# Low parts of the feed-forward activations on VectorE instead of GpSimd, and a lighter last group of block 1

## The chip, the cores and the metric

The kernel runs on one core of one Trainium2 chip. The metric is the device time of one execution in microseconds (us); a change is judged by the medians of runs before and after. The engines are named as in the profile: PE is TensorE (PEld its weight loads), DVE is VectorE, ACT is ScalarE, POOL is GpSimd, SP issues the DMAs. Each engine takes its own instructions strictly in the order in which they were written; engines wait for one another through semaphores.

## What is computed

Clustered attention (2 batches, 8 heads, 768 tokens, head size 64) gives x of 1536 tokens by 512. Two feed-forward blocks follow, and only these are touched:

```python
    x = np.ascontiguousarray(attn_out.transpose(0, 2, 1, 3)).reshape(B * S, H * D)
    x = _moe_ref(x=x, **moe_kwargs)          # block 1
    return _moe2_ref(x=x, **moe2_kwargs)     # block 2
...
    h = x @ w_in                                         # 512 -> 2048
    g = np.maximum(h, 0.0) + np.log1p(np.exp(-np.abs(h)))
    return (g @ w_out).astype(np.float32)                # 2048 -> 512
...
    g = x @ w_gate                                       # 512 -> 1536
    silu = g * (1.0 / (1.0 + np.exp(-g)))
    val = x @ w_val
    return (silu * val @ w_out).astype(np.float32)       # 1536 -> 512
```

## The kernel before

**Products in three passes.** A matrix product is made from operands split in a rounded high part and a low part (value minus high part): high by high, high by low, low by high, all added up in one PSUM bank. So each activation tile has a pair, gh and gl (block 1's g), YH and YL (block 1's output, which is block 2's input), ah and al (block 2's silu times val). The high part is a copy by ACT; the low part is a subtraction that must wait for that copy. Before the change gl and al (each 128x1536) are subtracted by POOL.

**Weights** come by DMA as 64-bit floats, in tiles of 128x512, and are narrowed to 32 bits and split: one ACT instruction (`m`, L123), then on DVE L125 and L128 (`m`), L132 and L135 (`m`), L148 (`whi`) and L149 (`wlo`). These steps lie as tasks in a list, `todo`; `pump()` emits one, two or three of them, by how many are left. There are two `m` buffers, so the ACT step of one weight waits for the `wlo` of the weight before the last. `need(...)` emits tasks until the named weight or activation is there.

**Block 1** has 16 units (`h_unit(f)`): 36 matmuls of 128x512 into three banks (L756), which ACT and DVE empty into `e` and `r` (L815, L819; L817 by DVE in units 0 to 2); then ACT's Exp and Ln (L822, L823), the sum `e` (DVE, L826), and the split into gh (ACT, L796) and gl (L797), these three as tasks in `todo`. After two units `y_group(g)` multiplies both by w_out (L845): four times (`d` from 0 to 3) 18 matmuls into three banks, which DVE adds to `acc` (L859; in the first group ACT copies them, L857), and a `pump()` after each `d`. In the last group each bank's result is also copied to YH (ACT, L861) and subtracted to YL (L863, by DVE or POOL).

**Block 2** has 12 units (`a_unit(f)`), with gate and val products (L756), and six `o_group`s (L944), emptied by DVE (L954, L956).

**Banks.** There are eight PSUM banks, used in turn, three for a unit or a `d`. So the third bank of a set is the one that was first in the set two sets before, and a set's third matmul waits until ACT or DVE has emptied that one (its first two banks were second and third in the set three sets before). The order of the code is the order on each engine.

Of the kernel before, what the change touches and what calls it, by code (L numbers as in the profile page):

```python
# [16 lines left out]
ALU = mybir.AluOpType  # L17
# [12 lines left out]
def _r(t):  # L30

    return t.bitcast(F32)
# [8 lines left out]
def kernel(  # L41
# [18 lines left out]
    nc = tc.nc  # L60
# [8 lines left out]
    KD = DM // 128  # L69
# [128 lines left out]
    def split_tasks(batch):  # L198

        steps = {}  # L200

        def first(key):
            while key not in loaded_t:
                load_ahead(len(loaded_t) + 1)
            steps[key] = w_narrow(loaded_t.pop(key))
            next(steps[key])

        def second(key):
            next(steps[key])

        def third(key, tag):
            x = next(steps[key])
            load_ahead(3)
            pool, bufs = pool_of[tag]
            W[key] = w_split(x, pool, tag, bufs)

        tasks = []
        for key, _, tag in batch:
            tasks.append(functools.partial(first, key))
            firsts.add(tasks[-1])  # L220
            tasks.append(functools.partial(second, key))
            begun.add(tasks[-1])
            tasks.append(functools.partial(third, key, tag))
            begun.add(tasks[-1])
        return tasks
# [11 lines left out]
    def pump(n=None):  # L237
        for _ in range(n or (3 if len(todo) > 12 else 2 if len(todo) > 4 else 1)):
            if todo and todo[0] in firsts:
                todo.popleft()()  # L240
            if todo:
                todo.popleft()()
            if todo and todo[0] in firsts and n is None:
                todo.popleft()()

    def need(table, key):
        while key not in table:
            todo.popleft()()
        return table[key]
# [393 lines left out]
    for half in range(2):  # L643
# [5 lines left out]
        for hh in range(2):  # L649
            g = 2 * C * hh  # L650
            if half == 0:
                nc.vector.tensor_scalar(
                    out=QT[hh][64:64 + C, 0, cols], in0=_r(ps)[g:g + C, 0:384], scalar1=FAR, scalar2=-FAR,
# [3 lines left out]
            else:  # L657
                nc.scalar.copy(KT[hh][64:64 + C, 0, cols], _r(ps)[64 + g:64 + g + C, 0:384])
                nc.scalar.activation(
                    out=QT[hh][64:64 + C, 0, cols], in_=_r(ps)[g:g + C, 0:384], func=AF.Identity,  # L660
# [84 lines left out]
    def bank():  # L745
        pool = bank_pools[bank_n[0] // 4 % len(bank_pools)]
        bank_n[0] += 1
        return pool.tile([128, 512], F32, tag="b", name="bank")

    def proj(xh, xl, w, banks, kks):  # L750

        hi, lo = w
        for kk in kks:
            for wt, xt, last in ((hi, xh, 0), (hi, xl, 0), (lo, xh, 1)):
                for c in range(NCH):
                    nc.tensor.matmul(  # L756
                        banks[c],
                        lhsT=wt[:, kk, :],
                        rhs=xt[:, kk, 512 * c:512 * c + 512],
                        start=(kk == 0 and wt is hi and xt is xh),  # L760
                        stop=(kk == KD - 1 and last == 1),
                    )
# [30 lines left out]
    def split_g(g, tag):  # L793
        gh = gp.tile([128, NTOK], F32R, tag="gh", name=tag + "h")
        gl = gp.tile([128, NTOK], F32R, tag="gl", name=tag + "l")
        nc.scalar.copy(gh, g)  # L796
        nc.gpsimd.tensor_tensor(out=gl, in0=g, in1=_r(gh), op=ALU.subtract)  # L797
        return gh, gl


# [32 lines left out]
    def y_group(g):  # L833
        last = g == NF1 // 2 - 1
        nd = 1
        for d0 in range(0, KD, nd):
            banks = [bank() for _ in range(nd * NCH)]
            for ff in range(2):
                hi, lo = need(W, ("out", 2 * g + ff))
                gh, gl = need(g_t, 2 * g + ff)  # L840
                for d in range(nd):
                    ds_ = slice(128 * (d0 + d), 128 * (d0 + d) + 128)
                    for n, (wt, gt) in enumerate(((hi, gh), (hi, gl), (lo, gh))):
                        for c in range(NCH):
                            nc.tensor.matmul(  # L845
                                banks[NCH * d + c],
                                lhsT=wt[:, 0, ds_],
                                rhs=gt[:, 512 * c:512 * c + 512],
                                start=(ff == 0 and n == 0),
                                stop=(ff == 1 and n == 2),  # L850
                            )
            for n, bk in enumerate(banks):
                d, c = d0 + n // NCH, n % NCH
                cs = slice(512 * c, 512 * c + 512)
                a = acc[:, d, cs]
                if g == 0:
                    nc.scalar.copy(a, bk)  # L857
                else:
                    nc.vector.tensor_tensor(out=a, in0=bk, in1=a, op=ALU.add)  # L859
                if last:  # L860
                    nc.scalar.copy(YH[:, d, cs], a)  # L861
                    eng = nc.gpsimd if c == 1 or c == 2 and d < KD - 1 else nc.vector
                    eng.tensor_tensor(out=YL[:, d, cs], in0=a, in1=_r(YH)[:, d, cs], op=ALU.subtract)  # L863
            pump()

    soft0, split0 = h_unit(0, h0)
    soft1, split1 = h_unit(1, h1)
# [2 lines left out]
    for g in range(NF1 // 2):  # L870
        if 2 * g + 2 < NF1:
            for f in (2 * g + 2, 2 * g + 3):
                soft, split = h_unit(f)
                if f < NF1 - 2:
                    todo.extend([soft[0]] + split[:3] + [soft[1]] + split[3:6] + [soft[2]] + split[6:])
                else:
                    first_do(soft + split[:3])
                    todo.extend(split[3:])
        else:
            YH = keep.tile([128, KD, NTOK], F32R, tag="xh", name="YH")  # L880
            YL = keep.tile([128, KD, NTOK], F32R, tag="xl", name="YL")
        y_group(g)
# [6 lines left out]
    def a_unit(f):  # L889
        gb = [bank() for _ in range(NCH)]  # L890
        wg = need(W, ("gate", f))
        vb = None
        if f == 0:
            vb = [bank() for _ in range(NCH)]
            wv = need(W, ("val", f))
            proj(YH, YL, wg, gb, range(KD - 1))
            proj(YH, YL, wv, vb, range(KD - 1))
            proj(YH, YL, wg, gb, range(KD - 1, KD))
            proj(YH, YL, wv, vb, range(KD - 1, KD))
        else:  # L900
            for half in range(2):
                proj(YH, YL, wg, gb, range(2 * half, 2 * half + 2))
                pump()
        sg = tp.tile([128, NTOK], F32, tag="e", name="sg")
        for c in range(NCH):
            cs = slice(512 * c, 512 * c + 512)
            nc.scalar.activation(out=sg[:, cs], in_=gb[c], func=AF.Silu)
        if vb is None:
            vb = [bank() for _ in range(NCH)]
            wv = need(W, ("val", f))  # L910
            for half in range(2):
                proj(YH, YL, wv, vb, range(2 * half, 2 * half + 2))
                pump()
        ah = gp.tile([128, NTOK], F32R, tag="gh", name="ah")
        al = gp.tile([128, NTOK], F32R, tag="gl", name="al")
        for c in range(NCH):
            cs = slice(512 * c, 512 * c + 512)
            nc.vector.tensor_tensor(out=sg[:, cs], in0=vb[c], in1=sg[:, cs], op=ALU.mult)  # L918
            if f == NF2 - 1:
                nc.scalar.copy(ah[:, cs], sg[:, cs])  # L920
                nc.vector.tensor_tensor(out=al[:, cs], in0=sg[:, cs], in1=_r(ah)[:, cs], op=ALU.subtract)

        def split_part():
            nc.scalar.copy(ah, sg)  # L924
            nc.gpsimd.tensor_tensor(out=al, in0=sg, in1=_r(ah), op=ALU.subtract)  # L925
            a_t[f] = (ah, al)

        if f < NF2 - 1:
            todo.append(split_part)
        else:  # L930
            a_t[f] = (ah, al)
        if batches:
            todo.extend(split_tasks(batches.pop(0)))

    def o_group(g):
        for t0 in range(0, NTOK // 128, 4):
# [22 lines left out]
            pump()  # L959

    a_unit(0)
    a_unit(1)
    for g in range(NF2 // 2):
        if 2 * g + 2 < NF2:
            a_unit(2 * g + 2)
            a_unit(2 * g + 3)
        o_group(g)
# [33 lines left out]
```

## Time and profile before

| what | us |
|---|---|
| median of 3 runs (lowest to highest) | 841.67 (839.91 to 848.4) |
| the profiled execution | 847.81 |
| its span, first to last instruction | 846.0 |

The profile is of one execution. Times in its rows count from the start of its span; block 1 lies from about 259 to 547 us and block 2 behind it. A row of an engine's time line gives the start, the duration, engine, line, operation, output and inputs, the count, and in brackets how long the engine had been idle before and who released it.

### The profile page before, as it was taken

The page shows a single profiled execution, that of the slowest core. Times are in us where ns is not written, and L with a number is a line of the kernel's source. Part 1 is how long each engine was busy: PE and PEld are TensorE (multiplying, and loading weights), DVE is VectorE, ACT ScalarE, POOL GpSimd, SP SyncE. Part 2 cuts the span into 40 slices and gives each one's busy share as a digit, 9 for nine tenths or more (in the row PEclk, how much of TensorE's full clock was granted, in tenths as well). Part 3 has the DMA queues.
Part 4 walks back from the last instruction along what each step waited for, and adds up shares of the span by engine and source line. Part 5 has one row for each costly group of instructions (what it writes and reads, how often), then busy time and mean ns, then how long its engine had stood idle before and what let it go on. Part 6 is the DMA issues. An engine that isn't in the chain of part 4 may idle for free.

```text
span 846.0 us, 11685 instructions
## 1 busy us (share of the span) xinstructions
PE 817.6 (97%) x4366; PEld 704.3 (83%) x4366; DVE 663.1 (78%) x1007; ACT 417.7 (49%) x774; POOL 240.7 (28%) x163
## 2 busy tenths in 40 slices
PE   7999999999999999999999999899999999999998
PEld 6999999999897778787787887688888888888886
DVE  6889988887895896989979789838885857766364
ACT  4589889888893776364553744233212112120210
POOL 4636455565421221212112313231111103011100
PEclk9699999999999989999999999999999999999999
DMA  8956765674411223122121120202311221310003
GB/s 213 262 134 143 197 148 147 147 170 113 103 31 54 75 75 100 50 77 74 60 90 51 50 76 26 74 1 78 121 52 49 76 74 50 100 51 25 1 1 149
DMA packets 65336, 75.42 MB, mean 89 GB/s; under 512 B 28960, under 2 KB 51584, under 8 KB 65280
## 3 DMA queue, kind: packets, MB, share of 16 engines
q1 hardware_dynamic: 65280, 74.68, 31.8%
q8 instruction: 34, 0.56, 0.3%
q14 instruction: 22, 0.18, 0.1%
HBM read 48.27 MB, written 3.19 MB: 61 GB/s over the span
## 4 chain that ended last, share of the span: by engine, by line
PE 75%; DVE 16%; DMA 4%; ACT 2%; issue 2%; POOL 1%; SPq 0%; POOLq 0%; DVEq 0%; ACTq 0%
PE bank L756 34%; PE bank L944 12%; PE bank L845 8%; PE ops L540 6%; PE sps L491 6%; PE tps L523 6%; DVE acc L859 3%; DVE whi L148 2%; DVE m L125 2%; PE sims L402 2%; DMA rd<-R 2%; DVE m L135 1%; DMA R<-rd 1%; DVE e L826 1%; DVE m L132 1%
## 5 line engine op out<-in xcount | busy, mean ns | idle before, releaser
L797 POOL TENSOR_TENSOR gl<-e,gh 128x1536 fp32r<-128x1536 f32 x16 | 59.9, 3746 | 204.7 <-ACT gh L796 191.6
L530 DVE TENSOR_TENSOR tl<-tps,th 128x384 fp32r<-128x384 f32 x192 | 98.8, 550 | 17.2 <-ACT th L529 16.8
L499 DVE TENSOR_REDUCE nm<-sps 128x1 f32<-128x768 f32 x96 | 91.4, 953 | 16.1 <-PE sps L491 13.3
L925 POOL TENSOR_TENSOR al<-sg,ah 128x1536 fp32r<-128x1536 f32 x11 | 38.6, 3507 | 207.0 <-ACT ah L924 207.0
L523 PE MATMUL tps<-id,p 128*128 128x128 f32 x576 | 95.4, 283 | 1.0 <-DVE tl L530 1.0
L529 ACT CAST th<-tps 128x384 fp32r<-128x384 f32 x192 | 84.7, 491 | 20.6 <-PE tps L523 18.0
L507 ACT ACTIVATE p<-sps,nm 128x768 f32<-128x768 f32 x96 | 88.3, 920 | 6.6 <-DVE nm L499 6.5
L491 PE MATMUL sps<-KT,QT 128*128 128x384 f32 x384 | 86.6, 348 | 4.1 <-ACT p L507 2.3
L756 PE MATMUL bank<-YH,whi 128*128 128x512 f32 x288 | 81.4, 390 | 3.3 <-DVE acc L859 3.3
L125 DVE TENSOR_SCALAR m<-m 128x512 f32<-128x512 f32 x68 | 58.9, 866 | 31.4 <-ACT m L123 31.3
L523 PEld LDWEIGHTS tps<-id,p 128*128 128x128 f32 x576 | 77.4, 154 | 7.2 <-DVE tl L530 3.4
L756 PE MATMUL bank<-YL,whi 128*128 128x512 f32 x288 | 81.5, 392 | 0.0
L756 PE MATMUL bank<-YH,wlo 128*128 128x512 f32 x288 | 81.4, 391 | 0.0
L540 PE MATMUL ops<-th,VV 128*128 128x256 f32 x288 | 80.6, 309 | 0.0
L123 ACT ACTIVATE m<-raw 128x512 f32<-128x512 f32 x68 | 44.5, 667 | 72.7 <-DVE wlo L149 72.7
L540 PE MATMUL ops<-tl,VV 128*128 128x256 f32 x288 | 73.1, 283 | 0.0
L918 DVE TENSOR_TENSOR sg<-bank,sg 128x512 f32<-128x512 f32 x36 | 22.8, 684 | 60.8 <-PE bank L756 60.8
L491 PEld LDWEIGHTS sps<-KT,QT 128*128 128x128 f32 x384 | 65.5, 196 | 5.4 <-ACT p L507 3.2
L845 PE MATMUL bank<-gh,whi 128*128 128x512 f32 x192 | 58.0, 407 | 11.0 <-DVE acc L859 6.6
L756 PEld LDWEIGHTS bank<-YH,whi 128*128 128x128 f32 x288 | 54.2, 188 | 15.0 <-issue 3.7
L756 PEld LDWEIGHTS bank<-YH,wlo 128*128 128x128 f32 x288 | 54.5, 189 | 11.4
L756 PEld LDWEIGHTS bank<-YL,whi 128*128 128x128 f32 x288 | 54.5, 189 | 11.3
(125 smaller groups left out, 1775.2 us busy)
## 6 DMA issues: line engine op xcount, KB each, us to landing
raw<-in_moe_w_out_dram SPq DMA_DIRECT2D x28, 512.0 KB, 3.4
raw<-in_moe_w_in_dram SPq DMA_DIRECT2D x16, 512.0 KB, 3.9
QT<-hi SPq DMA_DIRECT2D x32, 192.0 KB, 3.0
raw<-in_moe_w_val_dram SPq DMA_DIRECT2D x12, 512.0 KB, 3.9
raw<-in_moe_w_gate_dram SPq DMA_DIRECT2D x12, 512.0 KB, 3.4
KT<-hi SPq DMA_DIRECT2D x14, 384.0 KB, 4.9
qn<-in_q_dram SPq DMA_DIRECT2D x16, 192.0 KB, 4.4
kn<-in_k_dram SPq DMA_DIRECT2D x16, 192.0 KB, 4.0
```

The source lines that it names most:

```text
L125: nc.vector.tensor_scalar(out=m.bitcast(F32), in0=m.bitcast(F32), scalar1=F64_LEAST, scalar2=F64_MOST, op0=ALU.max, op1=ALU.min)
L491: nc.tensor.matmul(ps[:, c, 0:384], lhsT=Q[:, a, 128 * j:128 * j + 128], rhs=K[:, a, 384 * c:384 * c + 384], start=(a == 0), stop=(a == 1),)
L499: nc.vector.tensor_reduce(out=nm, in_=ps[:, :, 0:384], axis=AX.XY, op=ALU.max, negate=True)
L507: nc.scalar.activation(out=_h(p), in_=s_t.pop(i)[:, :, 0:384], func=AF.Exp, bias=nm_t.pop(i), accum_out=sm_t[pr][:, j:j + 1],)
L523: nc.tensor.transpose(ps[:, 128 * j:128 * j + 128], p[:, 128 * kb:128 * kb + 128], id32)
L529: nc.scalar.copy(th, pv)
L530: nc.vector.tensor_tensor(out=tl, in0=pv, in1=_r(th), op=ALU.subtract)
L540: nc.tensor.matmul(o[:, 0:CW], lhsT=VV_t[pr][:, hh, kb].rearrange("p a d -> p (a d)"), rhs=t[:, kb, :], start=(kb == 0 and lohi == 0), sto ...
L756: nc.tensor.matmul(banks[c], lhsT=wt[:, kk, :], rhs=xt[:, kk, 512 * c:512 * c + 512], start=(kk == 0 and wt is hi and xt is xh), stop=(kk ...
L797: nc.gpsimd.tensor_tensor(out=gl, in0=g, in1=_r(gh), op=ALU.subtract)
L845: nc.tensor.matmul(banks[NCH * d + c], lhsT=wt[:, 0, ds_], rhs=gt[:, 512 * c:512 * c + 512], start=(ff == 0 and n == 0), stop=(ff == 1 and ...
L944: nc.tensor.matmul(bk, lhsT=lhs[:, ts_], rhs=rhs[:, 0, :], start=(ff == 0 and n == 0), stop=(ff == 1 and n == 2),)
```

## The change

The two subtractions of gl and al go from POOL to DVE, at the same place in the code. In the last `y_group` no `pump()` is called, so nothing is narrowed there; `a_unit(0)` gets three `pump()`s between its products instead. And the subtraction that makes YL for one bank is emitted after the next bank has been added to `acc` and copied to YH, not right after its own.

```diff
         nc.scalar.copy(gh, g)
-        nc.gpsimd.tensor_tensor(out=gl, in0=g, in1=_r(gh), op=ALU.subtract)
+        nc.vector.tensor_tensor(out=gl, in0=g, in1=_r(gh), op=ALU.subtract)
...
         nd = 1
+        low = collections.deque()
...
                 if last:
                     nc.scalar.copy(YH[:, d, cs], a)
                     eng = nc.gpsimd if c == 1 or c == 2 and d < KD - 1 else nc.vector
-                    eng.tensor_tensor(out=YL[:, d, cs], in0=a, in1=_r(YH)[:, d, cs], op=ALU.subtract)
-            pump()
+                    low.append(functools.partial(
+                        eng.tensor_tensor, out=YL[:, d, cs], in0=a, in1=_r(YH)[:, d, cs], op=ALU.subtract
+                    ))
+                while len(low) > 1 or low and n == len(banks) - 1 and d0 == KD - nd:
+                    low.popleft()()
+            if not last:
+                pump()
...
             proj(YH, YL, wg, gb, range(KD - 1))
+            pump()
             proj(YH, YL, wv, vb, range(KD - 1))
+            pump()
             proj(YH, YL, wg, gb, range(KD - 1, KD))
             proj(YH, YL, wv, vb, range(KD - 1, KD))
+            pump()
...
             nc.scalar.copy(ah, sg)
-            nc.gpsimd.tensor_tensor(out=al, in0=sg, in1=_r(ah), op=ALU.subtract)
+            nc.vector.tensor_tensor(out=al, in0=sg, in1=_r(ah), op=ALU.subtract)
```

On DVE, in `y_group(1)` (banks of `d` 0, then of `d` 1 and 2), there stood before:

```order
L859 TENSOR_TENSOR acc<-bank,acc 128x512 x3
L826 TENSOR_TENSOR e<-r,e 128x1536
L125 TENSOR_SCALAR m<-m 128x512
L128 TENSOR_SCALAR m<-m 128x512
L132 SCALAR_TENSOR_TENSOR m<-raw,m 128x512
L135 SCALAR_TENSOR_TENSOR m<-raw,m 128x512
L148 CAST whi<-m 128x512
L149 TENSOR_TENSOR wlo<-m,whi 128x512
L859 TENSOR_TENSOR acc<-bank,acc 128x512 x3
L125 TENSOR_SCALAR m<-m 128x512
L128 TENSOR_SCALAR m<-m 128x512
L859 TENSOR_TENSOR acc<-bank,acc 128x512 x3
```

and after the change the stretch from the weight's last steps to the banks of `d` 2 reads:

```order
L148 CAST whi<-m 128x512
L149 TENSOR_TENSOR wlo<-m,whi 128x512
L860 TENSOR_TENSOR acc<-bank,acc 128x512 x3
L797 TENSOR_TENSOR gl<-e,gh 128x1536
L125 TENSOR_SCALAR m<-m 128x512
L128 TENSOR_SCALAR m<-m 128x512
L860 TENSOR_TENSOR acc<-bank,acc 128x512 x3
```

The gl of that unit now stands between the banks of `d` 1 and those of `d` 2; L859 has become L860.

On DVE in the last group, `y_group(7)`, there stood before, from the first bank of `d` 0 to the last YL:

```order
L859 TENSOR_TENSOR acc<-bank,acc 128x512 x2
L125 TENSOR_SCALAR m<-m 128x512
L128 TENSOR_SCALAR m<-m 128x512
L859 TENSOR_TENSOR acc<-bank,acc 128x512
L863 TENSOR_TENSOR YL<-acc,YH 128x512
L859 TENSOR_TENSOR acc<-bank,acc 128x512 x2
L132 SCALAR_TENSOR_TENSOR m<-raw,m 128x512
L135 SCALAR_TENSOR_TENSOR m<-raw,m 128x512
L148 CAST whi<-m 128x512
L149 TENSOR_TENSOR wlo<-m,whi 128x512
L859 TENSOR_TENSOR acc<-bank,acc 128x512
L863 TENSOR_TENSOR YL<-acc,YH 128x512
```

and now:

```order
L860 TENSOR_TENSOR acc<-bank,acc 128x512 x2
L868 TENSOR_TENSOR YL<-acc,YH 128x512
L860 TENSOR_TENSOR acc<-bank,acc 128x512 x3
L868 TENSOR_TENSOR YL<-acc,YH 128x512
L860 TENSOR_TENSOR acc<-bank,acc 128x512 x3
L868 TENSOR_TENSOR YL<-acc,YH 128x512
L860 TENSOR_TENSOR acc<-bank,acc 128x512 x3
L868 TENSOR_TENSOR YL<-acc,YH 128x512
L860 TENSOR_TENSOR acc<-bank,acc 128x512
L868 TENSOR_TENSOR YL<-acc,YH 128x512
L125 TENSOR_SCALAR m<-m 128x512
```

The six steps of one weight (the second gate tile, which `a_unit(1)` needs) have moved behind the whole group, and each YL stands one bank later. One weight load moves with them on SP's queue: `load_ahead` is called when a weight has been split. The order on PE and ACT is the same before and after.

## Rows read from the trace of the kernel before

**Rows 1.** The page: the chain that ended last, by engine

```profile
PE 75%; DVE 16%; DMA 4%; ACT 2%; issue 2%; POOL 1%; SPq 0%; POOLq 0%; DVEq 0%; ACTq 0%
```

**Rows 2.** Who PE waited for, 286 to 552: us in total, times, longest

```profile
PE bank L845 <- DVE acc L859: 6.6, 5, 1.8
PE bank L756 <- DVE acc L859: 4.2, 2, 3.3
PE bank L845 <- DVE r L817: 3.2, 1, 3.2
PE bank L845 <- DVE whi L148: 1.2, 1, 1.2
```

**Rows 3.** The chain in order of time, 286 to 552: start, us, what

```profile
298.14 19.07 PE bank L845 x70
317.21 16.32 PE bank L756 x72
...
348.04 5.53 PE bank L845 x16
...
384.43 3.92 PE bank L845 x16
...
422.39 16.16 PE bank L756 x70
...
453.05 5.52 PE bank L845 x16
...
547.27 4.76 PE bank L756 x14
```

**Rows 4.** The time line of PE, one of the waits

```profile
348.04 0.50 PE L845 MATMUL bank<-gh,whi 128*128 128x512 f32 x1 [1.82 <-DVE acc L859]
```

**Rows 5.** The time line of DVE, four places

```profile
297.41 1.87 DVE L817 TENSOR_SCALAR r<-bank 128x512 f32<-128x512 f32 x3
...
343.03 3.63 DVE L148 CAST whi<-m 128x512 fp32r<-128x512 f32 x1
...
347.31 1.88 DVE L859 TENSOR_TENSOR acc<-bank,acc 128x512 f32<-128x512 f32 x3
...
553.57 1.29 DVE L863 TENSOR_TENSOR YL<-acc,YH 128x512 fp32r<-128x512 f32 x1 [0.69 <-ACT YH L861]
```

**Rows 6.** The time line of POOL, three places

```profile
290.08 7.12 POOL L797 TENSOR_TENSOR gl<-e,gh 128x1536 fp32r<-128x1536 f32 x2 [30.82 <-ACT gh L796]
...
342.34 4.03 POOL L797 TENSOR_TENSOR gl<-e,gh 128x1536 fp32r<-128x1536 f32 x1 [9.31 <-ACT gh L796]
...
553.02 1.29 POOL L863 TENSOR_TENSOR YL<-acc,YH 128x512 fp32r<-128x512 f32 x1 [0.18 <-ACT YH L861]
```

**Rows 7.** Groups by line, 259 to 548 (last: 548 to 846): busy us, mean ns

```profile
L797 POOL TENSOR_TENSOR gl<-e,gh 128x1536 fp32r<-128x1536 f32 x16 | 59.9, 3746 | 204.7 <-ACT gh L796 191.6 <-PE bank L756 13.1
...
L826 DVE TENSOR_TENSOR e<-r,e 128x1536 f32<-128x1536 f32 x16 | 27.9, 1751 | 1.3 <-ACT e L823 1.3
...
L796 ACT CAST gh<-e 128x1536 fp32r<-128x1536 f32 x16 | 23.8, 1489 | 60.2 <-DVE e L826 60.2
...
L863 DVE TENSOR_TENSOR YL<-acc,YH 128x512 fp32r<-128x512 f32 x3 | 2.1, 692 | 2.1 <-ACT YH L861 2.1
...
L148 DVE CAST whi<-m 128x512 fp32r<-128x512 f32 x30 | 12.8, 427 | 1.0
```

**Rows 8.** The time line of ACT in `y_group(0)`

```profile
301.96 0.71 ACT L123 ACTIVATE m<-raw 128x512 f32<-128x512 f32 x1 [3.16 <-DVE wlo L149]
302.54 0.62 ACT L815 ACTIVATE e<-bank 128x512 f32<-128x512 f32 x1
```

**Rows 9.** Stretches: length, then busy of PE, PEld, DVE, ACT, POOL; clock, DMA

```profile
299.00:305.00 6.00, 6.00 (x16) 4.62 (x16) 5.45 (x11) 3.04 (x7) 0.00 (x0) 0.56 0.28 87
376.00:412.00 36.00, 34.18 (x152) 27.96 (x151) 33.07 (x40) 21.07 (x26) 10.46 (x3) 1.00 0.19 59
720.00:770.00 50.00, 50.00 (x222) 41.38 (x222) 35.32 (x57) 9.82 (x14) 7.03 (x2) 1.00 0.20 66
```

## The prediction, on record before the result

> **What bounds the kernel now.** I read first the chain that ended last [rows 1]: three quarters of it are PE and 16% are DVE, so PE is the bound and DVE delays it in places. The question is where, and whether the change touches those places. In block 2 the stretches show PE busy all the time, 50.00 of 50.00 us, with DVE at 35.32 [rows 9]: whatever al costs or saves there moves nothing as long as DVE keeps that slack. In block 1 PE does wait. The view of waits [rows 2] gives, from 286 to 552: 6.6 and 4.2 us for `acc` (a bank not yet emptied), 3.2 for `r`, 1.2 for `whi`: 15.2 us, all on DVE.
>
> Each wait costs more than its own length, which the chain shows [rows 3]. 72 matmuls of this shape take 16.32 us without a wait, 0.2267 each. The 16 that follow the wait at 348.04 [rows 4] take 5.53 instead of 3.63, so 1.90 are lost behind a wait of 1.82. In the same way 298.14 loses 19.07 - 70 x 0.2267 = 3.20, 384.43 loses 0.29, 422.39 0.29, 453.05 1.89, and 547.27 4.76 - 14 x 0.2267 = 1.59. The cause of the larger ones is the granted clock: 0.56 from 299 to 305, against 1.00 in the stretches around [rows 9], so PE stood at the lower of its two levels (1.2 instead of 2.4 GHz) for most of those 6 us, after 3.2 us of idling. Three shorter waits (525 to 540) I put at 0.3 each, by the rows that lose 0.29. Restarts cost 9.2 + 0.9 = 10.1 us. **So 25.3 us of block 1 are waits on DVE and their after-effects, and no more than about this can be won.**
>
> **Why DVE is late.** The mean of `whi` in block 2 is 427 ns [rows 7], but the one at 343.03 took 3.63 [rows 5]. POOL's gl beside it began at 342.34 and took 4.03 [rows 6]: it ended at 346.37, and `whi` at 346.66, 0.29 later. The same stands at 14 places of block 1 (also with L125 and L128, the other DVE steps with a single input): a copy-like step that should take 0.43 ends just behind POOL's subtraction. So DVE does not run beside gl, it is held by it, for 3.2 us each time. The Trainium skill (GPSIMD Engine Reference, section 8, Key points) says that POOL shares its SBUF interfaces with VectorE and contends with instructions in a two-port mode or with two SBUF inputs; by that rule every one of these holds goes with gl, and the trace agrees with 3.63 against 0.43 us.
>
> **gl on DVE.** It adds 16 subtractions of 128x1536. DVE has the same shape and number of inputs in `e`, 1751 ns [rows 7] (about 1.67 from one start to the next when they follow each other); POOL takes 3746. So 1.7 us come in and 3.2 of hold go out, 1.5 us less DVE work for each gl that now holds something. The wait that comes with it: gl needs gh from ACT (1489 ns, [rows 7]). In nearly all places the code leaves one weight's steps (3.4 us) or three banks (1.9) between `e` and gl on DVE, so gh is there by then.
>
> *The wait at 348.04.* PE wants the bank at 348.04 - 1.82 = 346.2. DVE reaches `whi` at 343.03; at 0.43 it is through at 343.5, `wlo` at 344.1, and the three additions, which began at 347.31 [rows 5], begin at 344.1, the first done at 344.8. The wait is gone with 1.4 us to spare. gl now stands behind them, before the banks of `d` 2: it delays those to 348.5, the first emptied by 349.2, and PE, which no longer stops, asks for it at 346.2 + 16 x 0.2267 + 0.5 = 350.3. Spare: about 1 us. The waits at 384.43 and 453.05 have the same order on DVE, and at 422.39 one held L125 precedes. All four go: 5.45 + 0.86 + 4.37 of restart = 10.7 us.
>
> *The wait at 298.14.* `r` starts at 297.41 [rows 5], right behind POOL's two gl, 290.08 to 297.20 [rows 6]. On DVE the first starts at 290.1, the second waits for its gh (1.5 later), is through at 293.3, two narrowing steps make it 294.2, and the first `r` is done by 294.9. PE wants it at 298.14 - 3.15 = 295.0. That wait goes, but a new one comes. The third bank of `d` 1 is the one that was unit 3's first, and ACT empties it only at 302.54, behind an L123 that waits for `wlo` [rows 8]. All of that moves with `r`, 3.2 earlier: L815 at 299.3, the bank free at about 300.5. PE wants it at 295.0 + 3.6 + 0.5 = 299.1. It waits 1.4, and restarts for between 0.3 and 1.9; I take 1.1. Of 6.35 us, 2.5 stay, 3.85 are won.
>
> **The last group.** The waits at 525 and 540 (6.6 - 5.45 = 1.2) and at 528 (1.2) lie behind held L125s. DVE gets through the two gl there 1.6 us earlier each; 1.2 + 1.2 + 0.9 = 3.3 go. At 547.27 PE waits 3.3 for the first bank of `d` 2 of the last group, which gate's third bank takes over. Before it DVE had six steps of a weight, two of them held by POOL's YL, and two YL that each wait 0.69 for ACT's YH. Without these, DVE empties each `d` as PE delivers it: three additions of 0.6 and one YL of 0.69 [rows 7], 2.5 us, against 18 x 0.2267 = 4.1 of PE. The bank is needed 18 matmuls and a half microsecond after PE has finished `d` 2, 4.5 us, and is emptied about 1 us after it. Even if a YL is held by POOL's, as the 1.29 at 553.57 beside POOL's 553.02 [rows 5, 6], twice 1.3 fits into the 3.5 left. So 3.3 + 1.6 = 4.9 go. The weight that moves is not needed until `a_unit(1)`, 72 matmuls (16 us) on; its 3.4 us on DVE lie beside PE's first products, and the DMA that moves with it feeds a value tile several units later. Nothing.
>
> **al.** 11 subtractions of 1.7 us on DVE, with up to 1.5 of waiting for ah where al stands right behind the product, against holds of up to 3.5 (POOL's 7.03 us there are two subtractions): at most two per 49 us, 6.4 us into a slack of 14.7 [rows 9]. What hides it is PE, busy 50 of 50. Without that cover it would be 11 x 1.7 = 19 us less what the holds give back. I take nothing.
>
> **The sum.** 10.7 + 3.85 + 3.3 + 4.9 = 22.75; I take 22.5. The profiled execution of 847.81 would become 825.3. It was 6.1 slower than the median of 841.67, and nothing in block 1 says why; so I put the same gain on the median: **819.2 us**, 2.7% faster.
>
> **Rivals.** *Half of it comes back.* The spare at the banks of `d` 2 is only 1 us, and gl stands before them. Were gl to wait there for gh (ACT's own queue holds it, in other groups, behind six steps that empty a unit's banks), a whole gh of 1.5 us would leave a wait of 0.5 and a restart of up to 1.9 in each of seven groups, some 11 to 12 us. For it: one queue, no slack of more than a microsecond. Against it: in the trace gh there starts right after `e`, before the weight's steps. It gives 841.67 - 11 = 830.5.
>
> *Slower.* The hold is not POOL's, or goes only in small part. Then every gl is added work: 33.07 us of DVE in 36.00 [rows 9] become 33.07 + 2 x 1.67 = 36.4, plus the up to 2.9 us that DVE stood idle, 36.4 to 39.3 for two units. Over seven pairs that is 3 to 23 us; in the middle +13, 854. It decides when a hold shrinks by less than the 1.67 that gl adds, about half. Against it speak 14 ends within some 0.3 us of POOL's.
>
> *No change.* The waits on `acc` go but PE's time is lost elsewhere in block 1, on ACT, as it does once at 298; about 840. The rows of waits show no other wait on ACT.
>
> **How the numbers follow.** Forecast 0.76, half 0.13, no change 0.06, slower 0.05. The range goes from 814 (all 25.3 won, from a median nearer to the lowest run, 839.91) to 831 (the half case) and leaves out the last two. A measurement of this kernel tells about 1%, 8.4 us, from no change; all of the forecast and nearly all of the half case are faster than that: 0.88; 0.07 within it, 0.05 slower.
>
> **What the profile after would show.** Right: gl of some 1.7 us on DVE; no `whi`, L125 or L128 over 0.5 us in block 1 except beside YL; PE's waits on `acc` gone at the four groups and at the head of block 2; one new wait of 1 to 2 us on ACT in `y_group(0)`; clock 1.00 from the second group on; block 2 no longer than before. Wrong: gl idling for gh, PE waiting for banks of `d` 2, or copies still held with POOL idle.

## The result, and the profile after

The changed kernel took 823.73 us in the median of 4 runs (822.62 to 825.85), the kernel before 841.6 (4 runs, 839.91 to 848.4): a ratio of 0.9755, 95% interval 0.9718 to 0.9791. That is 17.9 us less where 22.5 were forecast, inside the range. The profiled execution took 825.85, against 847.81 for the one before: 22.0 less, where the sum said 22.5.

The page after: the span, and the chain that ended last, by engine [rows 1].

```profile
span 824.1 us, 11644 instructions
...
PE 87%; DVE 6%; DMA 3%; ACT 1%; issue 1%; POOL 1%; SPq 0%; DVEq 0%; POOLq 0%; ACTq 0%
```

DVE's share of the chain fell from 16 to 6%, and what is left of it lies mostly ahead of 300 us. Who PE waited for, from 250 to 560 us, in block 1 (compare [rows 2]):

```profile
PE bank L846 <- ACT r L819: 1.2, 1, 1.2
...
PE bank L756 <- DVE whi L148: 0.7, 1, 0.7
```

None of the 15.2 us of waits on DVE that the prediction listed is left. The 0.7 for `whi` was there before at the same length; the prediction's list left it out, and it stood in no term of the sum. The 1.2 is the new wait on ACT that the prediction named. The chain from there on (start, us, what; compare [rows 3]):

```profile
302.12 12.09 PE bank L846 x52
314.20 16.32 PE bank L756 x72
...
526.45 18.59 PE bank L756 x82
```

From there to the end as one stretch (length, then busy of PE, PEld, DVE, ACT, POOL; clock, DMA):

```profile
302.00:824.00 522.00, 518.09 (x2284) 428.63 (x2284) 390.15 (x602) 182.19 (x251) 10.31 (x7) 1.00 0.20 65
```

Every 72 matmuls now take 16.32 us (16.41 in one place), from 314 into block 2: PE does not wait, and the granted clock of the stretch is 1.00. Behind the one wait the loss is 12.09 - 52 x 0.2267 = 0.30. The time line of DVE after, at the two places of [rows 5]:

```profile
291.72 3.42 DVE L797 TENSOR_TENSOR gl<-e,gh 128x1536 fp32r<-128x1536 f32 x2
...
295.85 1.88 DVE L817 TENSOR_SCALAR r<-bank 128x512 f32<-128x512 f32 x3
...
340.03 0.43 DVE L148 CAST whi<-m 128x512 fp32r<-128x512 f32 x1
...
341.10 1.88 DVE L860 TENSOR_TENSOR acc<-bank,acc 128x512 f32<-128x512 f32 x3
342.90 1.75 DVE L797 TENSOR_TENSOR gl<-e,gh 128x1536 fp32r<-128x1536 f32 x1
```

The `whi` that had taken 3.63 us takes 0.43, the three additions follow 1.1 later, and gl stands behind them. The groups after, 261 to 526 (busy us, mean ns, idle before; [rows 7]):

```profile
L797 DVE TENSOR_TENSOR gl<-e,gh 128x1536 fp32r<-128x1536 f32 x16 | 28.0, 1752 | 5.1 <-ACT gh L796 5.1
...
L148 DVE CAST whi<-m 128x512 fp32r<-128x512 f32 x35 | 15.0, 427 | 1.8
...
L125 DVE TENSOR_SCALAR m<-m 128x512 f32<-128x512 f32 x35 | 14.7, 421 | 9.6 <-ACT m L123 9.6
```

gl costs 1752 ns where 1751 was taken from `e`, and waits 5.1 us in all for gh. That idling costs nothing: PE does not wait for DVE there. On the two pages DVE's busy time falls from 663.1 to 641.9 us, although it has taken over 27 subtractions (1007 instructions before, 1034 after). The new wait, on ACT (compare [rows 8]) and then on PE:

```profile
300.42 0.67 ACT L123 ACTIVATE m<-raw 128x512 f32<-128x512 f32 x1 [1.46 <-DVE wlo L149]
300.99 0.58 ACT L815 ACTIVATE e<-bank 128x512 f32<-128x512 f32 x1
301.47 0.59 ACT L819 ACTIVATE r<-bank 128x512 f32<-128x512 f32 x1
```

```profile
302.12 0.50 PE L846 MATMUL bank<-gh,whi 128*128 128x512 f32 x1 [1.15 <-ACT r L819]
```

ACT stands in a narrowing step that waits for `wlo`, and unit 3's first bank is emptied behind it. In the last group, on DVE and on POOL:

```profile
518.51 0.69 DVE L868 TENSOR_TENSOR YL<-acc,YH 128x512 fp32r<-128x512 f32 x1
519.12 1.88 DVE L860 TENSOR_TENSOR acc<-bank,acc 128x512 f32<-128x512 f32 x3
521.09 1.29 DVE L868 TENSOR_TENSOR YL<-acc,YH 128x512 fp32r<-128x512 f32 x1
```

```profile
519.15 4.39 POOL L868 TENSOR_TENSOR YL<-acc,YH 128x512 fp32r<-128x512 f32 x3 [258.25 <-ACT YH L862]
```

The YL beside POOL's takes 1.29 instead of 0.69, as the prediction allowed for, and there is room for it. The three additions beside the same POOL step keep their 1.88.

To see where time went in each run, the span is cut at two rows of PE's time line: the first matmul of block 1 (L756 on XH) and the first of block 2 (L756 on YH).

| profile of | up to block 1 | block 1 | block 2 | span |
|---|---|---|---|---|
| before | 259.2 | 284.15 | 302.66 | 846.0 |
| control (before again) | 255.2 | 281.09 | 304.18 | 840.5 |
| after | 260.8 | 265.46 | 297.81 | 824.1 |
| again | 257.2 | 265.44 | 297.72 | 820.4 |
| again2 | 258.4 | 265.49 | 297.73 | 821.6 |
| gl_only | 258.8 | 265.74 | 303.01 | 827.5 |
| last_only | 258.4 | 278.98 | 297.78 | 835.2 |
| pool_too | 259.8 | 299.43 | 297.76 | 857.0 |
| narrow_stay | 259.1 | 265.77 | 301.99 | 826.9 |
| yl_now | 258.3 | 265.44 | 297.75 | 821.5 |
| al_pool | 259.8 | 265.47 | 297.74 | 823.0 |
| evac_first | 258.3 | 263.98 | 297.74 | 820.0 |
| evac_again | 260.3 | 264.02 | 297.77 | 822.1 |

From before to after, block 1 gave 18.7 us and the head of block 2 4.85, 23.5 together; 1.6 came back ahead of block 1, where nothing was changed and where one and the same kernel lies between 257.2 and 260.8. So it is partly luck that the two profiled executions differ by 22.0 where the sum said 22.5.

### The profile page after: what moved, and what is told of

It is laid out like the page before. It is cut to its first block, busy times and chain, and to the rows that moved or that the text cites. A ratio compares the mean times of both kernels' runs of the same rounds, so it can differ in the third digit from the quotient of the medians.

```text
span 824.1 us, 11644 instructions
## 1 busy us (share of the span) xinstructions
PE 808.5 (98%) x4366; PEld 699.6 (85%) x4366; DVE 641.9 (78%) x1034; ACT 416.8 (51%) x774; POOL 141.6 (17%) x136
## 4 chain that ended last, share of the span: by engine, by line
PE 87%; DVE 6%; DMA 3%; ACT 1%; issue 1%; POOL 1%; SPq 0%; DVEq 0%; POOLq 0%; ACTq 0%
PE bank L756 36%; PE bank L846 15%; PE bank L953 12%; PE sps L491 7%; PE ops L540 7%; PE tps L523 7%; PE sims L402 2%; PE mps L365 1%; DMA rd<-R 1%; DMA R<-rd 1%; DVE nm L499 1%; POOL xu L600 1%; DVE r L817 1%; DVE tl L530 1%; DMA KT<-khl 1%
## 5 line engine op out<-in xcount | busy, mean ns | idle before, releaser
L756 PE MATMUL bank<-YH,whi 128*128 128x512 f32 x288 | 80.8, 389 | 0.0
L756 PE MATMUL bank<-YL,whi 128*128 128x512 f32 x288 | 80.8, 389 | 0.0
L756 PE MATMUL bank<-YH,wlo 128*128 128x512 f32 x288 | 80.8, 389 | 0.0
L756 PEld LDWEIGHTS bank<-YH,whi 128*128 128x128 f32 x288 | 54.1, 188 | 11.2
L756 PEld LDWEIGHTS bank<-YL,whi 128*128 128x128 f32 x288 | 54.1, 188 | 11.2
L756 PEld LDWEIGHTS bank<-YH,wlo 128*128 128x128 f32 x288 | 54.1, 188 | 11.2
L933 ACT CAST ah<-sg 128x1536 fp32r<-128x1536 f32 x11 | 16.3, 1484 | 83.8 <-DVE sg L927 83.8
L916 ACT ACTIVATE sg<-bank 128x512 f32<-128x512 f32 x36 | 18.9, 599 | 76.1 <-PE bank L756 76.1
L953 PE MATMUL bank<-whi,ah 128*128 128x512 f32 x144 | 56.0, 389 | 0.0
L953 PE MATMUL bank<-wlo,ah 128*128 128x512 f32 x144 | 56.0, 389 | 0.0
```

Source lines behind the costliest of these rows:

```text
L756: nc.tensor.matmul(banks[c], lhsT=wt[:, kk, :], rhs=xt[:, kk, 512 * c:512 * c + 512], start=(kk == 0 and wt is hi and xt is xh), stop=(kk ...
L953: nc.tensor.matmul(bk, lhsT=lhs[:, ts_], rhs=rhs[:, 0, :], start=(ff == 0 and n == 0), stop=(ff == 1 and n == 2),)
```

## The experiments

The theory: POOL's gl holds DVE's steps, DVE empties banks late, PE waits and restarts at the lower clock; and the narrowing in the last group makes the wait at the head of block 2. The rivals: gl itself came too late from POOL; the lighter last group brings most of it; the clock, by chance, does.

**control**: the kernel before, unchanged.

> The kernel before, unchanged, to see which of its losses differ from one execution to the next. Theory (holds of VectorE by GpSimd's gl): the waits of PE in block 1 stand at the same places with the same lengths, 15 us in all, and only the matmuls at the lower clock behind them differ; so the time may lie anywhere between 839 and 848. Rival (the 6 us between the profiled execution and the median came from the attention part): the stretch up to 259 us is some us shorter than in the first profile, and block 1 is as long as there, 285 to 290 us.

One run: 842.32 us. PE's waits, and the chain of it:

```profile
PE bank L845 <- DVE acc L859: 6.6, 5, 1.8
PE bank L756 <- DVE acc L859: 4.1, 2, 3.3
PE bank L845 <- DVE r L817: 3.2, 1, 3.2
```

```profile
294.17 17.61 PE bank L845 x70
...
342.60 3.93 PE bank L845 x16
...
540.24 24.93 PE bank L756 x96
```

The waits are the same to a tenth. What follows them is not: the stretch behind the 3.2 us wait lost 17.61 - 70 x 0.2267 = 1.74 instead of 3.20, that behind the first 1.8 us wait 0.30 instead of 1.90, that at the head of block 2 24.93 - 96 x 0.2267 = 3.17 instead of 1.59 (over the whole run-up to full speed). The granted clock differs with it: behind the first 1.8 us wait it is 0.72 in the first profile and 1.00 in the control (one row of each):

```profile
348.00:354.00 6.00, 5.96 (x19) 4.74 (x20) 5.86 (x11) 0.09 (x1) 0.00 (x0) 0.72 0.00 0
```

```profile
342.00:348.00 6.00, 5.40 (x24) 4.47 (x25) 5.90 (x11) 0.65 (x1) 0.00 (x0) 1.00 0.00 0
```

The theory holds. Of the rival only the first half does: of the 5.5 us by which this span is shorter, 4.0 lie ahead of block 1, but block 1 itself is 3.1 shorter as well, and the head of block 2 is 1.5 longer. Measured against the control instead of the first profile, the two blocks gave 22.0 us instead of 23.5.

**gl_only**: gl and al on DVE, the last group as before.

```diff
-        nc.gpsimd.tensor_tensor(out=gl, in0=g, in1=_r(gh), op=ALU.subtract)
+        nc.vector.tensor_tensor(out=gl, in0=g, in1=_r(gh), op=ALU.subtract)
...
-            nc.gpsimd.tensor_tensor(out=al, in0=sg, in1=_r(ah), op=ALU.subtract)
+            nc.vector.tensor_tensor(out=al, in0=sg, in1=_r(ah), op=ALU.subtract)
```

> gl and al on VectorE, the last group as before. Theory: the waits on acc at the four groups, at 298 and at 525 to 528 go; the last group keeps a wait of 1 to 3 us at the head of block 2, since six narrowing steps and two 0.7 us waits for YH lie on VectorE there. 2 to 4 us more than the whole change: 825.5 to 828. Rival (most of the gain comes from the lighter last group): 834 or more.

828.25 us (6 runs) against 844.69 (17 runs) for before on that chip; ratio 0.9818 (0.9785 to 0.9851). PE's waits, and the chain at the head of block 2:

```profile
PE bank L756 <- DVE acc L859: 3.3, 1, 3.3
PE bank L845 <- ACT r L819: 1.1, 1, 1.1
```

```profile
528.43 36.59 PE bank L756 x153
```

All waits on `acc` but the last are gone with this edit alone, and the last is as long as before, 3.3 us, a little over the 1 to 3 expected; the time, too, is a little over its 825.5 to 828. With its restart (36.59 - 153 x 0.2267 = 1.91) it is 5.2 us: what this lacks against the whole change (303.01 - 297.8 in block 2).

**last_only**: the lighter last group, gl and al on POOL.

> The lighter last group alone, gl and al on GpSimd as before. Theory: only the wait at the head of block 2 with its restart goes, 3 to 5 us: 836 to 839; the four waits of 1.8 and 0.9 us and the one of 3.2 stay where they were. Rival (most of the gain comes from the lighter last group): 828 or less.

837.97 us (12 runs) against 844.69; ratio 0.9927 (0.9904 to 0.9949). PE's waits:

```profile
PE bank L846 <- DVE acc L860: 6.3, 4, 1.8
PE bank L846 <- DVE r L817: 3.2, 1, 3.2
PE bank L846 <- DVE whi L148: 1.2, 1, 1.2
PE bank L756 <- DVE acc L860: 0.8, 1, 0.8
```

Only the waits at the head of block 2 and of 0.4 within the last group are gone. So the lighter last group is the smaller part; the rival is out. The two parts make 16.4 + 6.7 = 23.1 by medians, the whole 21.8 (see again): they add up to within the spread of the times.

**again**: the whole change once more, on that chip.

> The whole change once more, on the same chip as its two parts. Theory: 822 to 826, PE waiting once in block 1 for ACT, 1.1 to 1.2 us, and at full clock from there on. Rival (the clock after waits is what differs by chance): the time moves with the clock in block 1, by up to 4 us from run to run.

822.9 us (6 runs) against 844.69; ratio 0.9757 (0.9721 to 0.9793). Block 1 is as long as in the first profile to 0.02 us. In all three profiles of the change it is 265.44 to 265.49, so the gain of block 1 is not made by the clock by chance. By these medians the gain is 21.8. Of the 3.9 us that the first set's 17.9 lacks, 3.1 lie in its median of before (841.6 from 4 runs spread over 8.5; three later sets, each on another chip, gave 844.69, 842.77 and 844.4).

**pool_too**: the whole change, and POOL does each subtraction of block 1 as well, into a tile that nobody reads.

```diff
+    spare = mp.tile([128, NTOK], F32R, tag="spare", name="spare")
...
         nc.vector.tensor_tensor(out=gl, in0=g, in1=_r(gh), op=ALU.subtract)
+        nc.gpsimd.tensor_tensor(out=spare, in0=g, in1=_r(gh), op=ALU.subtract)
```

> The whole change, but GpSimd does each of block 1's 16 subtractions as well, into a spare tile that nobody reads: the hold without the lateness. Theory (GpSimd's subtraction holds VectorE): narrowing steps of 3 us or gl itself of 2.5 to 3.5 us beside it, VectorE about 36 us busy in the 33 that two units take PE, PE's waits on acc back and longer: 836 to 856. Rival (gl came too late from GpSimd, and the stretched steps did not matter): gl is on time here, so 822 to 826.

856.21 us (4 runs) against 842.77 (11 runs): ratio 1.0157 (1.0126 to 1.0188), slower than before and just above the 836 to 856 expected. DVE's and POOL's time lines at the place of [rows 5], two units as a stretch (length, busy of PE, PEld, DVE, ACT, POOL, clock, DMA), and PE's waits:

```profile
347.31 3.61 DVE L148 CAST whi<-m 128x512 fp32r<-128x512 f32 x1
...
353.36 1.75 DVE L799 TENSOR_TENSOR gl<-e,gh 128x1536 fp32r<-128x1536 f32 x1
```

```profile
346.69 3.94 POOL L800 TENSOR_TENSOR spare<-e,gh 128x1536 fp32r<-128x1536 f32 x1 [8.65 <-ACT gh L798]
```

```profile
379.00:415.00 36.00, 34.19 (x152) 27.97 (x151) 35.18 (x43) 16.99 (x22) 7.94 (x2) 1.00 0.22 71
```

```profile
PE bank L849 <- DVE acc L863: 15.5, 7, 3.2
PE bank L849 <- DVE r L820: 6.5, 1, 6.5
```

The hold is back, 3.61 for 0.43, ending at 350.92 behind POOL's 350.63. gl is made by DVE here and used from there, so its lateness on POOL cannot be the cause, and no wait in [rows 2] is on gl; a subtraction on POOL that no one needs is enough. DVE is busy 35.18 of 36 us. POOL's extra reading also makes ACT wait for `e` three times, 6.5 us in all, but none of PE's waits there is on ACT.

**narrow_stay**: the whole change, but the second gate tile is narrowed in the last group again.

```diff
-            if not last:
-                pump()
+            pump()
...
             proj(YH, YL, wg, gb, range(KD - 1))
-            pump()
             proj(YH, YL, wv, vb, range(KD - 1))
-            pump()
             proj(YH, YL, wg, gb, range(KD - 1, KD))
             proj(YH, YL, wv, vb, range(KD - 1, KD))
-            pump()
```

> The whole change, but the narrowing of the second gate tile stays in the last group (the low parts of the output one bank later, as in the change). Theory (the narrowing, half held by GpSimd's YL, makes the wait at the head of block 2): PE waits 1 to 3 us there and loses up to 2 more behind it, 824.5 to 828. Rival (it is the waits of YL for YH): no wait, 822 to 824.

827.21 us (4 runs) against 842.77; ratio 0.9811 (0.9782 to 0.984). PE's wait there, the chain behind it, and DVE's steps:

```profile
PE bank L756 <- DVE acc L860: 2.4, 1, 2.4
```

```profile
527.90 47.23 PE bank L756 x200
```

```profile
518.05 1.01 DVE L125 TENSOR_SCALAR m<-m 128x512 f32<-128x512 f32 x1
519.10 1.40 DVE L128 TENSOR_SCALAR m<-m 128x512 int32<-128x512 int32 x1
...
523.00 1.27 DVE L132 SCALAR_TENSOR_TENSOR m<-raw,m 128x512 int32<-128x512 int32 x1
524.30 1.66 DVE L135 SCALAR_TENSOR_TENSOR m<-raw,m 128x512 int32<-128x512 int32 x1
```

POOL's steps beside them:

```profile
517.48 2.73 POOL L868 TENSOR_TENSOR YL<-acc,YH 128x512 fp32r<-128x512 f32 x2 [258.27 <-ACT YH L862]
522.43 2.99 POOL L868 TENSOR_TENSOR YL<-acc,YH 128x512 fp32r<-128x512 f32 x2 [2.21 <-ACT YH L862]
```

Four of the six steps are stretched beside POOL's YL. A wait of 2.4 with its restart (47.23 - 200 x 0.2267 = 1.9) is back. Whether the narrowing would have fitted without the stretching was not tried.

**yl_now**: the whole change, but each YL right after its own bank.

```diff
-                while len(low) > 1 or low and n == len(banks) - 1 and d0 == KD - nd:
+                while low:
                     low.popleft()()
```

> The whole change, but each low part of the output is made right after its own bank again; the narrowing stays out of the last group. Theory: VectorE needs 3.1 us for three banks where PE needs 4.1, no wait at the head of block 2, 822 to 826, as the whole change. Rival (it is the waits of YL for YH): a wait of 1 to 3 us there, 825 to 828.

822.69 us (4 runs) against 842.77; ratio 0.9753 (0.9725 to 0.978), and no wait at the head of block 2 (297.75 us). The later YL is worth nothing once the narrowing has moved; beside the narrowing it is worth 0.9 us of wait (3.3 in gl_only, 2.4 in narrow_stay).

**evac_first** and **evac_again**: the whole change, but unit 3's second `pump()` comes after its banks have been emptied.

```diff
                 proj(XH, XL, w, banks, range(2 * half, 2 * half + 2))
-                pump()
+                if f != 3 or half == 0:
+                    pump()
...
                 nc.scalar.activation(out=r[:, cs], in_=banks[c], func=AF.Relu)
+        if f == 3:
+            pump()
```

> The whole change, with unit 3's second pump emitted after its banks are emptied, so that ScalarE empties them before the narrowing step that waits for VectorE. Theory (that step's wait is what delays the bank): PE's one wait of 1.15 us at 300 to 302 goes, with 0.3 of restart: 1.4 us less, which the times may not tell. Rival (ScalarE is late for another reason): the wait stays, or another of the same size takes its place.

> The version with unit 3's banks emptied first, beside the whole change on the same chip. Theory: 1.4 us less than the whole change, 0.17%, within the noise of the times; in the profile block 1 is 1.4 shorter from its first matmul to block 2's first. Rival (the 2 us less seen before are the chip's spread): no difference in the profile's block 1.

820.72 us (6 runs) against 842.77, ratio 0.9731 (0.9703 to 0.9759); and 822.42 (6 runs) against 844.4, ratio 0.9735 (0.9697 to 0.9774), where the whole change took 823.27. ACT in evac_first:

```profile
296.31 0.58 ACT L816 ACTIVATE e<-bank 128x512 f32<-128x512 f32 x1
296.79 0.59 ACT L820 ACTIVATE r<-bank 128x512 f32<-128x512 f32 x1
...
299.18 0.70 ACT L123 ACTIVATE m<-raw 128x512 f32<-128x512 f32 x1
```

The bank is emptied first, PE's wait on ACT is gone, and block 1 is 264.0 us in both profiles instead of 265.45: the 1.45 us of wait and restart. By the profile it is the fastest version; the times cannot tell 0.2%.

**al_pool**: the whole change, but al stays on POOL.

> The whole change, but block 2's al stays on GpSimd. Theory (block 2 is bound by PE and VectorE has slack there): no wait of PE, block 2 from its first matmul to the end 297.7 to 297.9 us as in the whole change, 821 to 826. Rival (part of the gain is al's): VectorE late by 3 us holds per subtraction, PE waits on banks in block 2, 825 to 835.

822.54 us (6 runs) against 844.4; ratio 0.9748 (0.9712 to 0.9784). A group of block 2, and one `wlo` of it with POOL's al:

```profile
L149 DVE TENSOR_TENSOR wlo<-m,whi 128x512 fp32r<-128x512 f32 x30 | 27.1, 904 | 1.0
```

```profile
561.36 3.87 DVE L149 TENSOR_TENSOR wlo<-m,whi 128x512 fp32r<-128x512 f32 x1
```

```profile
561.13 3.55 POOL L934 TENSOR_TENSOR al<-sg,ah 128x1536 fp32r<-128x1536 f32 x1 [12.74 <-ACT ah L933]
```

DVE is held here too (904 ns on average for a `wlo` that takes 693 after the change), and PE does not wait once: block 2 is 297.74 us. al is worth nothing. `wlo` has two inputs, so the hold is not confined to the steps with a single input that the prediction named.

**again2**: the whole change, for the last two.

> The whole change, for those two. Theory: 821 to 826; block 1, from its first matmul to block 2's first, 265.4 to 265.5 us as in the two profiles before. Rival (the length of block 1 varies by chance): more than 1 us off that.

823.27 us (6 runs) against 844.4; ratio 0.975 (0.9712 to 0.9788). Block 1 is 265.49 us, within the 265.4 to 265.5 expected.

## Why the prediction was right, and where its sizes were off

*The bound.* Right. 15.2 us of waits on DVE and what followed them were put down as all that could be won, and nearly all of it came: block 1 and the head of block 2 gave 23.5 of 25.3 in the first pair of profiles. Most of the rest is the new wait on ACT with its restart, 1.45.

*The hold.* Right, and shown from both sides: without a subtraction on POOL `whi` and L125 average 427 and 421 ns; with a useless one the 3.6 us are back and the kernel is 13 us slower than before. That run has the load of DVE that the rival "slower" describes, the gl and the hold together. Its price was put at 3 to 23 us, +13 in the middle, and 13.4 came; a hit this close on so wide a range is luck. The Trainium skill (GPSIMD Engine Reference, section 8, Key points) counts instructions with two SBUF inputs among those that contend as well; the trace agrees, with 1.29 for 0.69 us of a YL and 1.66 for 0.69 of L135.

*The wait at 298.* The mechanism was right, its size off: 1.4 of wait and 1.1 of restart were put down to the new wait on ACT, 1.15 and 0.30 were measured. That is 1.05 us more gain than the sum had, and more than covers the difference between 22.75 and 23.5. evac_first shows that the cause is the narrowing step ahead of that bank on ACT.

*The last group.* 4.9 were forecast at the head of block 2, 4.85 came. That it is so close is luck in part: against the control 6.4 came and against gl_only 5.2, since the restart differs from one profile to the next. The cause was named too broadly: the prediction counted the narrowing and the waits of YL for YH together. narrow_stay and yl_now show that PE waits there only when the narrowing stays in the group, and that the order of the YLs adds 0.9 to such a wait; gl_only shows that the wait there keeps its full length when gl has gone.

*al.* Nothing was forecast, nothing came.

*From the profile to the median.* This term was off, within the range. The 22.5 of the profile were put on the median of 841.67 with the remark that nothing in block 1 said why the profiled execution was 6.1 slower. Something did: the control had the same waits but lost 1.5 us less in the two blocks, with a granted clock of 1.00 instead of 0.72 behind one of them. That is a part only. The medians of later sets (11 to 17 runs of before) give a gain of 21.8 and 21.1. Of the 3.7 us by which the second measurement of the change (822.9) lies above the 819.2 forecast, 3.0 are the median of before (844.69 instead of 841.67) and 0.7 the gain. Before varies more widely (839.9 to 849.3 in all sets) than the whole change (821.8 to 825.9), and the record says with what: of the 39 runs of before in the three later sets, the 18 with a mean granted clock up to 0.986 took 846.7 us on average and the 21 above it 842.3, and the profiled execution had 0.980. That the clock goes with the time is shown so; what makes it differ from one execution to the next is not.

*The rivals.* "Half of it comes back" did not happen: gl waited 5.1 us for gh in all, none of it ahead of a bank that PE wanted. "No change" did not happen either: the one wait on ACT was 1.15 us.

## What to carry to other kernels

When an engine's short steps have a long tail (0.43 and 3.6 us for the same shape), look at what the neighbour was doing at the moment when they end; if they end together with its instruction, compare what the work costs there with its length on the late engine: here a hold of 3.2 us against 1.75. Count with a wait of TensorE also what follows it, since it may be as long as the wait. And before giving a change its credit, undo its parts one by one: here one of four edits (gl to DVE) brought about three quarters, one (the narrowing out of the last group) about a quarter, and two (al, and the later YL once the narrowing had moved) nothing.

## What was not expected of the hardware

The cost of a wait's aftermath differs from one execution to the next: 16 matmuls behind the same wait of 1.8 us took 5.53 us in one profile of before and 3.93 in another, where 3.63 is full speed. And the restart at the head of block 2 cost 1.59, 3.17, 1.9 and 1.9 us behind waits of 3.3, 3.3, 3.3 (gl_only) and 2.4 (narrow_stay). The profiles of the whole change have one such wait, of 1.1 to 1.2 us, and it cost 0.30 to 0.33 in each of the three. What decides the cost of a restart was not tried.

A held step lasts until POOL's instruction ends, however short it is alone: a `whi` of 0.43 us took 3.63 and ended 0.29 behind POOL's gl, a `wlo` of 0.69 took 3.87 and ended 0.55 behind POOL's al. The additions that take a bank as one input were not stretched beside POOL's YL. No run was made to tell the two apart.
